# FFN2 of batches 5 and 6 by seven block products

## The chip, the cores and the metric

The kernel runs on one core of a Trainium2 chip. The time is microseconds (us) of one execution on the device; lower is better. The profile and the trace show one profiled execution, in which times count from the first instruction. Engines: PE multiplies matrices (PEld is its load of weights), DVE and ACT work on rows in on-chip memory and read PE's accumulators, POOL works on rows too but not on accumulators, SP issues output transfers.

## The reference

Inputs are q, k, v (8 batches x 8 heads x 576 x 64) and phi (8 x 8 x 576 x 32), and four weights. For each batch and head:

```python
a = softmax(phi, axis=2)                 # over the 576 rows
k_m, v_m = a.T @ k, a.T @ v              # 32 x 64
attn = softmax(q @ k_m.T / sqrt(64))     # 576 x 32
x = attn @ v_m                           # heads side by side: 4608 x 512 over all batches
h = maximum(maximum(x @ w1, x @ w2), x @ w3)   # 4608 x 768
out = h @ w_out                          # 4608 x 512
```

## The kernel before

All arithmetic on PE is in bf16 with 32-bit accumulators; outputs are 32-bit. The product with v_m is folded into the weights of each batch: `wp` holds v_m times (w1 - w3) and v_m times (w2 - w3), and `wp3` holds v_m times w3 times w_out. So h is kept as a difference to x @ w3 (`hT`, 768 columns in six tiles of 128, two batches side by side), and FFN2 adds attn @ wp3 to h @ w_out.

The order of all work is written out by hand: the long string that ends the kernel lists pieces such as F8@4, and each engine runs its own share of them in that order. The letter is the step, the number behind it the part, and the number behind @ the batch. A "!" swaps the engine of the step.

- L0 to L3 and H load phi, k, v and q; the issue is on POOL. E exponentiates phi on ACT. r0 and r1 (`pack`, L103) copy k and v from `kvo` into `kvr` beside a column of ones, on POOL, from batch 2 on.
- B (`att_kv`, L249) makes the key and value sums, N scales them on DVE, K transposes them. Q transposes q on DVE. S (`att_score`) makes the scores and two exponentials on ACT.
- a, s, c (DVE), m (POOL, `att_mul`, L409) and X (DVE) normalise the scores, in halves 0 and 1; X writes `attn`.
- D (`fold`, L440) folds v_m into the weights, in the parts 0 to 2 for `wp` and 3 for `wp3`; ACT or DVE takes the result out of the accumulators.
- F (`ffn1`, L466) is one of 12 pieces of FFN1 of a batch, four matmuls of 288 columns: an even number makes `h1` (evicted on ACT, L170), an odd one the other difference, which DVE joins to `h1` by a maximum into `hT` (L479).
- T0 to T3 (`ffn2`, L497 and L506) are tiles of 128 rows of a batch's output, T4 the 128 rows that two batches share, 64 of each. A tile is six matmuls of 512 columns on `hT` and two on `attn`, an eviction into `ot`, one of six buffers, and a transfer of 256 KB that SP issues. The last tile, T3@7, is made in two halves of 256 columns (`ffn2_last`, L538 and L546).

The eight banks of accumulators are dealt out by a second string of digits. A piece that gets a bank waits until its last user has been evicted.

Of the kernel before, what the change touches and what calls it, by code (L numbers as in the profile page):

```python
# [15 lines left out]
def kernel(  # L16
# [12 lines left out]
    nc = tc.nc  # L29
# [33 lines left out]
    kvos = []
    for i in range(2):
        kvo = const.tile([P, 3, NP, NC, D], BF16, name=f"kvo{i}")
        kvos.append(kvo)
# [28 lines left out]
    def load_kv(b, i, h=slice(0, NP)):
        kv = loaded.setdefault(b, {})["kv"] = kvos[b % 2]
        nc.gpsimd.dma_start(  # L97
            out=kv[:, 1 - i, h].rearrange("p j c d -> p j (c d)"),
            in_=by_pair((k, v)[i], b)[:, h],
        )  # L100

    def pack(b, i):
        nc.gpsimd.tensor_copy(  # L103
            out=kvrs[b % 2][:, :, :, D * i : D * (i + 1)], in_=kvos[b % 2][:, 1 - i]
        )
# [32 lines left out]
    banks = iter(  # L138
        "".join(
            """  # L140
            00224460026701101401264026402640264026452063420643064206420642064562074206742064
            20642064201640264102640264026402640264072406247026402640264024602406520462046204
            62704267402640264124602416420642064206420642067676767670
            """.split()
        )
    )
# [81 lines left out]
            s["e"] = work.tile([P, NP, NC, M], BF16, name="e")  # L228
        nc.scalar.activation(out=s["e"][:, js], in_=loaded[b]["ph"][:, js], func=AF.Exp)  # L229

    def k_and_ones(kv, r, j, c):

        flat = kv[r].rearrange("p i j c d -> p (i j c d)")
        k0 = (NP * NC + j * NC + c) * D
        step = 2 * NP * NC * D - k0
        return flat[:, k0 : k0 + 2 * step].rearrange("p (i x) -> p i x", i=2)[:, :, 0:D]

    def att_kv(b, part=None):
        s = st[b]
        kvp = two_banks()  # L240
        s["kvp", part] = kvp
        kv = loaded[b]["kv"]
        nd = {None: 2 * D + 1, 0: 2 * D, 1: D}[part]
        kvr = kvrs[b % 2]
        for c in range(NC):
            for j in range(NP):
                for a in range(NG):
                    r = slice(HP * a, HP * (a + 1))
                    nc.tensor.matmul(  # L249
                        kvp[M * j : M * (j + 1), a, 0:nd],  # L250
                        lhsT=s["e"][r, j, c, :],
                        rhs={
                            None: lambda: kvr[r, j, c, 0:nd],
                            0: lambda: k_and_ones(kv, r, j, c),
                            1: lambda: kv[r, 0, j, c, :],
                        }[part](),
                        start=(c == 0),
                        stop=(c == NC - 1),
                        tile_position=(HP * a, M * j),
                    )  # L260
# [102 lines left out]
    def ones_rec(b, g):  # L363
# [39 lines left out]
        s = st[b]  # L403
        nc.vector.reciprocal(out=s["sm", g], in_=s["sm", g])  # L404

    def att_mul(b, g):
        s = st[b]
        t = s["t", g]
        nc.gpsimd.tensor_tensor(  # L409
            out=t,  # L410
            in0=t,
            in1=s["sm", g].unsqueeze(2).to_broadcast([P, S // HP, R, 2]),
# [43 lines left out]
    def ffn1(b, n, swap):  # L456
# [20 lines left out]
        else:  # L477
# [83 lines left out]
    def issue(b, n, swap):  # L561
# [18 lines left out]
            "m": lambda: att_mul(b, i),  # L580
# [11 lines left out]


    for w in """
        E@0 H2@0 H0@0 L3@0 Z25@0 B0@0 Y2@0 I@0 N0@0 Z2@0 K0@0! Q0@0 Q1@0 Z9@0 S@0 Z2@0 M0@0 M1@0
        R0@0 R1@0 W0@0 Y3@0 W1@0 W2@0 Z6@0 O1@0 H3@0 O3@0 O2@0 H1@0 X1@0 B1@0 X0@0 N1@0
        K1@0 O0@0 Y0@0 D1@0! D0@0! D3@0 F8@0 F10@0 F2@0 V0@0 F6@0 F0@0! Y1@0 D2@0 D4@0 F4@0
        L0@1 V1@0 F1@0 E@1 F3@0 L1@1 F5@0 F9@0 F7@0 L3@1 F11@0 B0@1 T3@0 N0@1 K0@1! L2@1 Q1@1
        L2@2 L1@2 Q0@1 L0@2 V2@0 T0@0! L3@2 S@1 T1@0 a0@1 s0@1 c0@1 m0@1 B1@1 N1@1 a1@1 L1@3
        K1@1 s1@1 D0@1 D1@1! D2@1 c1@1 m1@1 X0@1 L3@3 r1@2 X1@1 T2@0! L2@3 F6@1 F10@1 F7@1 F2@1  # L600
        F3@1 F4@1 F0@1 r0@2 E@2 F5@1 F1@1 F11@1 L0@3 L0@4 F8@1 L2@4 F9@1 B@2 D3@1 N@2 Q1@2
        T0@1! K@2 T2@1! r0@3 Q0@2 S@2 a0@2 a1@2 s1@2 c1@2 m1@2 T4@1! D1@2! s0@2 D2@2 c0@2 m0@2
        X1@2 D0@2 T3@1 Q0@3 L3@4 X0@2 Q1@3 T1@1 F0@2 F4@2 F8@2 F6@2 F9@2 E@3 F7@2 r1@3 F5@2
        F10@2 F1@2 B@3 L1@4 D3@2 N@3 L0@5 F2@2 F11@2 E@4 F3@2 L1@5 K@3 r1@4 L2@5 T2@2! S@3 T3@2
        a0@3 s0@3 c0@3 m0@3 D0@3 D2@3 a1@3 s1@3 c1@3 X0@3 D1@3! Q0@4 m1@3 T1@2 L3@5 L2@6 T0@2!
        X1@3 F10@3 r0@4 F2@3 F4@3 E@5 Q1@4 r0@5 F5@3 F3@3 L1@6 F8@3 B@4 N@4 D3@3 F9@3 F6@3
        F11@3 L0@6 K@4 F0@3 F7@3 F1@3 S@4 a0@4 T4@3! s0@4 a1@4 D0@4 c0@4 s1@4 r1@5 c1@4 D3@4
        m0@4 X0@4 Q0@5 T0@3! D1@4! D2@4 B@5 T3@3 m1@4 X1@4 L0@7 F10@4 Q1@5 N@5 F8@4 K@5 F6@4
        F9@4 S@5 F7@4 L3@6 F2@4 F4@4 a0@5 L1@7 a1@5 F0@4 s0@5 r1@6 F3@4 D0@5 r0@6 s1@5 c1@5 E@6
        D3@5 m1@5 c0@5 F1@4 T1@3 L2@7 F11@4 L3@7 E@7 F5@4 m0@5 B@6 D1@5! D2@5 X1@5 N@6 T2@3!  # L610
        X0@5 F6@5 F8@5 Q0@6 Q1@6 K@6 F4@5 F9@5 S@6 F7@5 r0@7 a0@6 F2@5 a1@6 s0@6 c0@6 F0@5
        F10@5 m0@6 F1@5 s1@6 c1@6 F11@5 F5@5 T0@4! F3@5 X0@6 T2@4! r1@7 D0@6 D1@6! Q0@7 B@7
        m1@6 N@7 X1@6 T2@5! K@7 T3@4 Q1@7 S@7 a0@7 F2@6 s0@7 a1@7 s1@7 c1@7 m1@7 c0@7 F4@6
        T4@5! D3@6 D2@7 D0@7! T0@5! D3@7 D2@6 X1@7 m0@7 D1@7! T1@4 X0@7 F6@7 F3@6 T1@5 F4@7
        F8@7 F0@7 F5@6 F10@6 F7@7 F9@7 F10@7 F5@7 F0@6 F11@7 F6@6 F1@7 F7@6 F2@7 F8@6 F11@6
        F9@6 F1@6 F3@7 T0@6! T0@7! T3@5 T2@7! T2@6! T1@6 T1@7 T3@6 T4@7! T3@7
    """.split():
        n, b = w.rstrip("!").split("@")
        issue(int(b), n, w.endswith("!"))
# [30 lines left out]
```

## Time and profile before

| | us |
|---|---|
| median of 3 runs | 164.66 |
| lowest and highest run | 164.32, 165.99 |
| profiled execution, first to last instruction | 163.3 |
| PE busy | 153.8 |
| ACT busy | 100.6 |
| DVE busy | 90.4 |
| POOL busy | 69.5 |

A line of a group has the source line, the engine, the operation with its output and inputs, how many there were, then busy time in all and the mean of one in ns. "min/median/max" lines give ns of one. In the chain of waits a line is a start, a duration and what ran: the chain is followed back from the last instruction, at each step to what released it. Positions in the text are us from the first instruction.

### The profile page before, as it was taken

To read this page: it belongs to the slowest core of one execution; us is meant where nothing else is said; L and a number is where in the kernel's file an instruction comes from. 1 tells how busy PE (TensorE), PEld (TensorE's weight loads), DVE (VectorE), ACT (ScalarE), POOL (GpSimd) and SP (SyncE) were. 2 spreads that over 40 slices of the span, in tenths; PEclk is the share of its full clock that TensorE was granted. 3 is DMA by queue.
4 is the path that set the end of the run, shared out by engine and by line. 5 is a ranking of instruction groups with operands and counts; after the bars stand their busy time and mean duration, and the time that the engine had idled before them with its cause. 6 is when DMAs were issued, how large, how long until landed. Compare 5 with 4: busy or idle time off the path is not lost.

```text
span 163.3 us, 4838 instructions
## 1 busy us (share of the span) xinstructions
PE 153.8 (94%) x2080; PEld 85.3 (52%) x2080; DVE 90.4 (55%) x181; ACT 100.6 (62%) x151; POOL 69.5 (43%) x71
## 2 busy tenths in 40 slices
PE   7978798899899999999999999999999999999990
PEld 2433444564377436743673575576553468744450
DVE  2023704798838665849399748879749128810010
ACT  4205445845497488778885899994658976223320
POOL 7932205100599259657968957646403100000000
PEclk9999999999999999999999999999999999999998
DMA  6999999999999999999999999996313130014333
GB/s 150 152 206 207 205 210 217 274 208 210 253 313 238 209 253 379 274 210 293 252 263 206 232 355 264 191 233 150 130 69 129 69 128 0 0 68 186 135 128 130
DMA packets 21974, 31.77 MB, mean 195 GB/s; under 512 B 1216, under 2 KB 16576, under 8 KB 21952
## 3 DMA queue, kind: packets, MB, share of 16 engines
q0 software_dynamic: 16080, 21.43, 68.7%
q1 hardware_dynamic: 5728, 9.90, 17.2%
q8 instruction: 16, 0.26, 0.6%
q10 hardware_dynamic: 144, 0.13, 0.2%
q14 instruction: 6, 0.05, 0.1%
HBM read 39.32 MB, written 9.44 MB: 299 GB/s over the span
## 4 chain that ended last, share of the span: by engine, by line
PE 83%; DMA 9%; POOL 2%; ACT 2%; issue 1%; DVE 1%; ACTq 0%; POOLq 0%
PE psum L497 29%; PE psum L466 28%; DMA wo_sb<-in_moe_w_out_dram 9%; PE psum L506 8%; PE psum L440 6%; PE psum L249 4%; PE psum L192 3%; PE psum L333 2%; PE psum L515 1%; ACT h L170 1%; PE psum L538 1%; PE psum L298 1%; POOL kvo L97 1%; ACT wp L172 1%; POOL qq L110 0%
## 5 line engine op out<-in xcount | busy, mean ns | idle before, releaser
L497 PE MATMUL psum<-wo_sb,hT 128*128 128x512 bf16 x210 | 51.3, 380 | 0.0
L466 PE MATMUL psum<-attn,wp 128*128 128x288 bf16 x384 | 50.5, 286 | 0.1
L479 DVE TENSOR_TENSOR hT<-psum,h 128x576 bf16<-128x576 f32 x48 | 34.2, 749 | 18.0 <-PE psum L466 12.5
L466 PEld LDWEIGHTS <-wp 128*128 128x128 bf16 x384 | 36.7, 98 | 13.2 <-issue 2.0
L172 ACT COPY ot<-psum 128x512 f32<-128x512 f32 x35 | 20.7, 591 | 32.1 <-PE psum L506 25.2
L497 PEld LDWEIGHTS <-hT 128*128 128x128 bf16 x210 | 19.2, 97 | 24.0 <-issue 4.3
L172 ACT CAST wp<-psum 128x1024 bf16<-128x1024 f32 (+1 forms) x31 | 29.2, 995 | 3.8 <-PE psum L440 2.0
L103 POOL COPY kvr<-kvo 128x2304 bf16<-128x2304 bf16 x12 | 25.3, 2111 | 13.7 <-DMA kvo<-in_k_dram 10.1
L170 ACT ACTIVATE h<-psum 128x576 bf16<-128x576 f32 x47 | 28.4, 659 | 3.5 <-PE psum L466 3.3
L409 POOL TENSOR_TENSOR t<-t,sm 128x576 bf16<-128x576 bf16 x14 | 16.1, 1154 | 24.6 <-DVE sm L404 24.4
L506 PE MATMUL psum<-wp,attn 128*128 128x512 bf16 x62 | 18.4, 379 | 0.0
L159 PE MATMUL psum<-warm 128*128 128x512 bf16 x44 | 12.1, 427 | 1.2 <-DVE warm L128 1.2
L313 DVE STREAM_TRANSPOSE qT<-qq 128x576 f32<-128x576 f32 x16 | 11.7, 747 | 1.4 <-DMA qq<-in_q_dram 1.4
L342 ACT ACTIVATE e<-psum 128x576 bf16<-128x576 f32 x16 | 9.6, 652 | 3.8 <-PE psum L333 3.8
L229 ACT ACTIVATE e<-ph 128x1152 bf16<-128x1152 f32 (+1 forms) x9 | 9.6, 1065 | 1.7 <-DMA ph<-in_phi_dram 1.6
L395 DVE TENSOR_REDUCE sm<-t 128x18 f32<-128x576 bf16 x14 | 10.3, 738 | 0.2
L387 DVE STREAM_TRANSPOSE t<-e 128x288 f32<-128x288 f32 x14 | 6.4, 465 | 6.2 <-ACT e L342 6.1
L97 POOL DMA_DIRECT2D kvo<-in_v_dram x9 | 6.7, 749 | 7.1 <-PE psum L249 4.1
L506 PEld LDWEIGHTS <-attn 128*128 128x128 bf16 x62 | 6.1, 98 | 7.1
L110 POOL DMA_DIRECT2D qq<-in_q_dram x8 | 6.2, 770 | 6.6 <-DVE h L174 3.7
L555 DVE COPY ot<-psum 128x256 f32<-128x256 f32 x1 | 0.4, 425 | 15.4 <-PE psum L546 15.4
L249 PEld LDWEIGHTS <-e 64*32 64x32 bf16 x720 | 6.9, 90 | 3.7 <-issue 3.3
(57 smaller groups left out, 114.4 us busy)
## 6 DMA issues: line engine op xcount, KB each, us to landing
out_dram<-ot SPq DMA_DIRECT2D x35, 256.0 KB, 5.6
qq<-in_q_dram POOLq DMA_DIRECT2D x8, 576.0 KB, 12.2
ph<-in_phi_dram POOLq DMA_DIRECT2D x7, 576.0 KB, 14.4
kvo<-in_k_dram POOLq DMA_DIRECT2D x7, 576.0 KB, 14.6
kvo<-in_v_dram POOLq DMA_DIRECT2D x7, 576.0 KB, 15.6
w_sb<-in_moe_w_dram POOLq DMA_DIRECT2D x3, 768.0 KB, 19.0
wo_sb<-in_moe_w_out_dram POOLq DMA_DIRECT2D x1, 768.0 KB, 14.6
ph<-in_phi_dram SPq DMA_DIRECT2D x2, 288.0 KB, 3.0
```

What stands on the lines that cost most here:

```text
L103: nc.gpsimd.tensor_copy(out=kvrs[b % 2][:, :, :, D * i : D * (i + 1)], in_=kvos[b % 2][:, 1 - i])
L159: nc.tensor.matmul(po[:, 0:BANK], lhsT=warm[:, 0:P], rhs=warm, start=True, stop=True)
L170: nc.scalar.activation(out=out_, in_=in_, func=AF.Relu)
L172: nc.scalar.copy(out=out_, in_=in_)
L249: nc.tensor.matmul(kvp[M * j : M * (j + 1), a, 0:nd], lhsT=s["e"][r, j, c, :], rhs={None: lambda: kvr[r, j, c, 0:nd], 0: lambda: k_and_one ...
L313: nc.vector.transpose(out=s["qT"][:, j].rearrange("p j c r e -> p (j c r e)").bitcast(FP32), in_=loaded[b]["q"][:, j].rearrange("p j c d - ...
L395: nc.vector.tensor_reduce(out=sm, in_=s["t", g].rearrange("p n r e -> p n e r"), op=ALU.add, axis=mybir.AxisListType.X,)
L409: nc.gpsimd.tensor_tensor(out=t, in0=t, in1=s["sm", g].unsqueeze(2).to_broadcast([P, S // HP, R, 2]), op=ALU.mult,)
L466: nc.tensor.matmul(acc[:, h, 0:SH], lhsT=wps[b][:, g, w * DF + ft * P : w * DF + (ft + 1) * P], rhs=attn[:, g, c0 : c0 + SH], start=(g == ...
L479: nc.vector.tensor_tensor(out=hT[:, ft, (b % 2) * S : (b % 2 + 1) * S].rearrange("p (h n) -> p h n", h=2), in0=a, in1=s["h1", ft], op=ALU.max,
L497: nc.tensor.matmul(po, lhsT=hT[:, fc, c0 : c0 + P], rhs=wo_sb[:, fc, :], start=(n == 0), stop=False,)
L506: nc.tensor.matmul(po, lhsT=attn[:, g, c0 : c0 + P], rhs=wp3s[b][:, g, :], start=False, stop=(g == NG - 1),)
```

## The change

For batches 5 and 6 the tiles T0 to T3 go. Their 512 rows by 512 columns are taken as two by two blocks: rows in the two parities r of 128-row tiles (256 rows each), columns in halves of 256, and the inner dimension in two halves of four tiles, three of h and one of attn. Seven products of blocks, in place of eight, give the four blocks of the output, with sums and differences of blocks of h and attn (A) and of the weights (U) made beforehand. U@9 makes those of w_out once, in the room of `w3T`; U@5 and U@6 make those of `wp3`, which differ by batch. The sums of h lie in the room of w3 and, for A2, in `hT` itself; A0 to A3 are those of h (768 columns), A4 to A7 those of attn (256).

A product P is eight matmuls of 256 columns, for two row tiles into the halves of one bank. Three banks are used for a batch: P1, P4, P5 and P6 add up in one, P0 and P3 in another, and P2 has the third. After P0, P1 and P4 a copy of the bank is kept (`snap`, 512 columns of 32 bits), and the output is one plain copy and three adds of a bank and a snapshot on DVE, into `oj0` and `oj1`, of 512 KB each, which one transfer each takes out.

Beside this, the pack can be made on ACT (used for r1@7), A runs on DVE without "!" and on POOL with it, U the other way round, output buffers `ot` fall from six to four, `kvo` loses an unused third, the string of banks is new, and the order is new from the piece after F7@2 on. Before that it is the same.

```diff
-    opool = ctx.enter_context(tc.tile_pool(name="opool", bufs=6))
+    opool = ctx.enter_context(tc.tile_pool(name="opool", bufs=4))
...
-    def pack(b, i):
-        nc.gpsimd.tensor_copy(
-            out=kvrs[b % 2][:, :, :, D * i : D * (i + 1)], in_=kvos[b % 2][:, 1 - i]
-        )
+    def pack(b, i, swap):
+        out_, in_ = kvrs[b % 2][:, :, :, D * i : D * (i + 1)], kvos[b % 2][:, i]
+        if swap:
+            nc.scalar.copy(out=out_, in_=in_)
+        else:
+            nc.gpsimd.tensor_copy(out=out_, in_=in_)
...
+    SNAP = {0: "m5", 1: "m1", 4: "u2"}
...
+    def combine(on_dve, out_, in0, in1, op):
+        eng = nc.vector if on_dve else nc.gpsimd
+        eng.tensor_tensor(out=out_, in0=in0, in1=in1, op=op)
+
+    def combine_w(b, i, on_dve):
...
+        in0, in1 = [(x[B12], x[B11]), (x[B22], t[0]), (x[B22], x[B12]), (x[B21], t[1])][i]
+        combine(on_dve, t[i], in0, in1, SUB)
...
+    def combine_a(b, i, on_dve):
+
+        s, sa = sums(b)
+        n = i % 4
+        if i < 4:
+            (a11, a12), (a21, a22) = blocks(hts[b // 2], b, KT)
+            t = {0: s[:, 0], 1: s[:, 1], 2: a21, 3: s[:, 2]}
+        else:
+            (a11, a12), (a21, a22) = blocks(attns[b // 2], b, 1)
+            t = {m: sa[:, m : m + 1] for m in range(4)}
+        in0, in1 = [(a21, a22), (t[0], a11), (a11, a21), (a12, t[1])][n]
+        combine(on_dve, t[n], in0, in1, ADD if n == 0 else SUB)
+
+    def products(b, i, swap):
...
+        lhs, rhs, name = [
+            (summed(0), w_summed(0), "y"),
+            (plain(0, 0), w_plain(0, 0), "x"),
+            (plain(0, 1), w_plain(1, 0), "z"),
+            (summed(3), w_plain(1, 1), "y"),
+            (summed(1), w_summed(1), "x"),
+            (summed(2), w_summed(2), "x"),
+            (plain(1, 1), w_summed(3), "x"),
+        ][i]
...
+        for k in range(KT + 1):
+            for q in range(2):
+                nc.tensor.matmul(
+                    po[:, q * CH : (q + 1) * CH],
+                    lhsT=lhs(k, q),
+                    rhs=rhs(k),
+                    start=(i < 3 and k == 0 and q == 0),
+                    stop=(k == KT and q == 1),
+                    skip_group_check=True,
+                )
...
+        if i in SNAP:
+            t = ln if i == 0 else work.tile([P, S], FP32, name="snap", tag="r")
+            t = acc[SNAP[i]] = t[:, 0:DM].rearrange("p (q n) -> p q n", q=2)
+            copy(t, x)
...
+        done = [2] if i == 2 else [i] if i > 4 else [4] if 3 in acc and 4 in acc else []
+        for n in done:
+            ot = acc["ot"][n // 5][:, :, slice(0, CH) if n in (2, 6) else slice(CH, DM)]
+            if n == 6:
+                copy(ot, x)
+            else:
+                if n == 4:
+                    x = acc["y"].rearrange("p (q n) -> p q n", q=2)
+                y = acc[{2: "m1", 4: "u2", 5: "m5"}[n]]
+                nc.vector.tensor_tensor(out=ot, in0=x, in1=y, op=ADD)
+            if n in (4, 6):
...
+                nc.sync.dma_start(out=rows[:, :, n // 5], in_=acc["ot"][n // 5])
...
-            "r": lambda: pack(b, i),
+            "r": lambda: pack(b, i, swap),
...
+            "U": lambda: combine_w(b, i, swap),
+            "A": lambda: combine_a(b, i, not swap),
+            "P": lambda: products(b, i, swap),
...
+        Q1@3 T1@1 F0@2 F4@2 F8@2 F6@2 F9@2 E@3 F7@2 F1@2 L1@4 r1@3 F10@2 F2@2 L2@5 B@3
+        N@3 D3@2 F3@2 L1@5 F5@2 K@3! U0@9 F11@2 S@3 U1@9 E@4 T3@2 L0@5 T0@2! a1@3 D1@3!
+        s1@3 D2@3 a0@3 r1@4 c1@3 L3@5 D0@3 T1@2 m1@3 s0@3 Q0@4 X1@3 c0@3 m0@3 X0@3 T2@2!
+        F4@3! r0@4 F5@3 L2@6 F0@3 D3@3 B@4 F6@3 N@4 F1@3 F8@3 Q1@4 F2@3 F9@3 K@4! F10@3
+        r1@5 F7@3 S@4 F11@3 L3@6 D3@4 E@5 r0@5 F3@3 a0@4 U3@9 L0@6 a1@4 T4@3! L1@6 L0@7
+        s1@4 D0@4 D1@4! B@5 c1@4 N@5 T1@3 Q1@5 K@5 L1@7 Q0@5 s0@4 c0@4 m0@4 T3@3! S@5
+        a0@5 T2@3! s0@5 a1@5 c0@5 X0@4 m1@4 X1@4 D2@4 D0@5 D1@5 m0@5 s1@5 X0@5 T0@3!
+        F4@4 c1@5 F2@4 m1@5 r1@6 L2@7 F10@4 r0@6 F3@4 F5@4 F8@4 X1@5 F9@4 F0@4 F11@4
+        F6@4 E@6 F10@5! F7@4 L3@7 F0@5 F2@5 A4@5! Q0@6 A5@5! F1@4 F1@5 A7@5! F8@5 F6@5
+        F4@5! Q1@6 D3@5 B@6 N@6 r0@7 D2@5 T0@4! F7@5 F5@5 K@6 F3@5 U2@9 F9@5 U0@5! T1@4!
+        F11@5 A0@5 A6@5 r1@7! E@7 S@6 T2@4! D1@6! U1@5! D2@6 a0@6 Q1@7 B@7 A1@5! U2@5
+        U3@5 N@7 T3@4 s0@6 K@7! Q0@7 a1@6 P1@5 D3@6 s1@6 c1@6 S@7 c0@6 A2@5! m1@6 P2@5
+        P4@5 a0@7 s0@7 D3@7 D2@7 m0@6 a1@7 c0@7 D1@7! P0@5! A3@5! U0@6 s1@7 P5@5 c1@7
+        m1@7 X1@6 X0@6 T4@5! D0@6! D0@7 P6@5 U1@6 m0@7 F8@6 F9@6 F6@6 U3@6 U2@6 X0@7
+        P3@5 F10@6 F2@6 X1@7 F11@6 F8@7 F0@6 F3@6 F7@6 F4@7 F1@6 F9@7 F4@6 A4@6 F5@6
+        F2@7 F0@7 F5@7 A0@6! A6@6! A1@6! F6@7 F10@7! F3@7 A5@6! P1@6 A2@6! F1@7 P0@6
+        F7@7 A3@6! F11@7 P2@6! P4@6 T0@7 T1@7 P5@6! A7@6 T4@7 P6@6! P3@6! T2@7! T3@7
```

More of the change, by code (lines that the diff above doesn't have):

```diff
@@ L62 @@
     nc.scalar.preload_act_table_set("natural_log_exp_and_others")
[L63 to L66, printed above, removed]
+    KV = NP * NC * D
+    ones_k = [const.tile([P, D + 2 * KV], BF16, name=f"kvo{i}") for i in range(2)]
+    kvos = [
+        x[:, D:].rearrange("p (i j c d) -> p i j c d", i=2, j=NP, c=NC) for x in ones_k
+    ]
     kvrs = [
@@ L128 @@
     nc.vector.memset(warm, 0.0)
-    for kvo in kvos:
-        nc.vector.memset(kvo[:, 2, 0, 0], 1.0)
+    for x in ones_k:
+        nc.vector.memset(x[:, 0:D], 1.0)
     blkones = const.tile([P, P], BF16, name="blkones")
@@ L280, in att_kv_norm @@
             return
+        k0 = D if part == 0 else 0
         for g in range(NG):
@@ L370, in ones_rec @@
         )
-        r = work.tile([P, S], FP32, name="r")
+        r = work.tile([P, S], FP32, name="r", tag="r")
         nc.scalar.activation(out=r, in_=ln, func=AF.Exp, scale=-1.0)
@@ L484, in ffn1 @@
             )
+    KT = FT // 2
+    CH = DM // 2
+    TW = 2 * P
+    SUB, ADD = ALU.subtract, ALU.add
+    B11, B12, B21, B22 = [
+        (slice(KT * i, KT * (i + 1)), slice(CH * j, CH * (j + 1)))
+        for i in range(2)
+        for j in range(2)
+    ]
+    tw = w3T.rearrange("p f j n -> p (f j n)").rearrange("p (i k c) -> p i k c", i=4, k=KT)
+    sa0 = const.tile([P, 4, TW], BF16, name="sa0")
+    oj0 = [const.tile([P, 2, DM], FP32, name=f"oj{i}") for i in range(2)]
+    SNAP = {0: "m5", 1: "m1", 4: "u2"}
@@ new lines @@
+    twb, sas, quads = {}, {}, {}
+    def combine(on_dve, out_, in0, in1, op):
+        eng = nc.vector if on_dve else nc.gpsimd
+        eng.tensor_tensor(out=out_, in0=in0, in1=in1, op=op)
+    def combine_w(b, i, on_dve):
+        if b == B + 1:
+            x = {n: wo_sb[:, n[0], n[1]] for n in (B11, B12, B21, B22)}
+            t = [tw[:, n] for n in range(4)]
+        else:
+            if b not in twb:
+                twb[b] = work.tile([P, 4, CH], BF16, name="twb")
+            w = wp3s[b]
+            x = {n: w[:, n[0].start // KT, n[1]] for n in (B11, B12, B21, B22)}
+            t = [twb[b][:, n] for n in range(4)]
+        in0, in1 = [(x[B12], x[B11]), (x[B22], t[0]), (x[B22], x[B12]), (x[B21], t[1])][i]
+        combine(on_dve, t[i], in0, in1, SUB)
@@ L601 @@
[L601 to L612, printed above, removed]
```

118 lines of the change are left out of this document (90 added, 28 removed).

## Prediction

> **What bounds the kernel now.** I read the page's summary first, then the chain of waits in order of time, then the busy time by stretches, and last the queues that the change loads. The page says one engine is nearly full, and the chain says the end follows that engine:
>
> ```profile
> span 163.3 us, 4838 instructions
> PE 153.8 (94%) x2080; PEld 85.3 (52%) x2080; DVE 90.4 (55%) x181; ACT 100.6 (62%) x151; POOL 69.5 (43%) x71
> PE 83%; DMA 9%; POOL 2%; ACT 2%; issue 1%; DVE 1%; ACTq 0%; POOLq 0%
> ```
>
> A busy PE need not be PE at its limit, so the pieces of the chain matter more (start, duration, what):
>
> ```profile
> 28.96 1.75 ACT h L170 x3
> ...
> 43.23 0.17 DVE kvt L176
> 43.41 0.04 issue
> 43.45 0.84 PE psum L440 x24
> ...
> 81.78 0.73 PE psum L249 x71
> 82.51 0.23 PE psum L440 x8
> ...
> 84.32 0.17 PE psum L298 x3
> ...
> 85.95 0.41 PE psum L333 x23
> ...
> 91.47 0.65 PE psum L249 x69
> 92.12 1.40 PE psum L497 x6
> 93.52 0.43 PE psum L506 x2
> ...
> 100.27 1.29 PE psum L497 x6
> 101.57 0.43 PE psum L506 x2
> ...
> 116.63 0.65 PE psum L249 x69
> ...
> 132.27 9.80 PE psum L466 x80
> ...
> 157.18 0.55 PE psum L515 x4
> 157.73 0.76 PE psum L538 x6
> 158.49 0.22 PE psum L546 x2
> 158.71 0.66 PE psum L538 x6
> ```
>
> From 43.45 on the chain holds PE work alone, but for one 0.02 us of issue. Each piece starts where the last ended. Waits of other engines lie before that, where the order of pieces isn't changed. By stretches (length, then busy time of each engine and its instructions, clock, DMA share, GB/s):
>
> ```profile
> 70.00:115.00 45.00, 44.98 (x685) 25.95 (x684) 34.63 (x72) 36.31 (x53) 32.17 (x26) 1.00 1.11 238
> 115.00:159.60 44.60, 44.58 (x412) 24.24 (x410) 17.54 (x32) 23.86 (x37) 3.42 (x4) 1.00 0.26 98
> 159.60:163.30 3.70, 0.00 (x0) 0.00 (x0) 0.00 (x0) 0.37 (x1) 0.00 (x0) 0.78 0.32 109
> ```
>
> PE is full in both, at clock 1.00. In 70 to 115 DVE, ACT and POOL have 20 to 30% left and DMA none; after 115 all four have room. So less PE work shortens the run, as long as nobody else falls behind in 70 to 115.
>
> **The products on PE.** FFN2 of one 128-row tile is six matmuls on h and two on attn, 1.29 + 0.43 = 1.72 us; the 1.40 stands where a piece follows matmuls of 64 rows, and the 0.11 more is the price of entry. The change takes out four such tiles in each of batches 5 and 6: 8 x 1.72 = 13.76 us. It puts in 14 products of eight matmuls of 256 columns. The trace has that very form, in the last tile, which is made in halves: 0.66 + 0.22 = 0.88 us for eight, 110 ns each, each with a weight load of its own. 14 x 0.88 = 12.32 us, so PE loses 1.44 us. Seven products in place of eight leave 7/8 of the columns; of the time 12.32 / 13.76, 0.895, are left, so the smaller matmuls give little of it back. Entries: in both orders 27 runs of narrow matmuls (key sums, scores, folds) are followed by full ones, so none is gained or lost.
>
> To place pieces in the new order I add prices along it: an FFN1 piece 0.49 (9.80 for twenty), a tile 1.72, the shared one of two batches 1.29 + 0.55 = 1.84, a product 0.88, key sums 0.73, a fold 0.23, scores 0.41, transposes 0.17, and 0.11 for each entry. Only differences of such sums are used below.
>
> [...]
>
> **What the products need from the others.** Prices, from the forms:
>
> ```profile
> L103 POOL COPY kvr<-kvo x12: 2102/2108/2124, 46.4 to 112.9; 128x2304 bf16<-128x2304 bf16 x12
> L409 POOL TENSOR_TENSOR t<-t,sm x14: 1147/1152/1174, 42.4 to 126.2; 128x576 bf16<-128x576 bf16 x14
> L377 DVE TENSOR_TENSOR attn<-e,r x2: 749/750/751, 18.4 to 19.1; 128x576 bf16<-128x576 bf16 x2
> L479 DVE TENSOR_TENSOR hT<-psum,h x48: 694/748/758, 32.7 to 142.6; 128x576 bf16<-128x576 f32 x48
> L172 ACT COPY ot<-psum x35: 585/586/632, 37.7 to 157.8; 128x512 f32<-128x512 f32 x35
> L229 ACT ACTIVATE e<-ph 128x1152 bf16<-128x1152 f32 x7 | 8.2, 1174 | 0.0
> ```
>
> Evictions: a batch had four copies of 586 ns; it gets three snapshots and one plain copy of that size, so nothing is added there, and three adds on DVE, by L479 0.748 x 512/576 = 0.67 us each, 2.0 us a batch. Most lie after 115, where DVE is busy 17.54 of 44.60. They stand on PE's path only where a product adds onto a bank that is still being read. In batch 5, P4 follows P1's snapshot with a fold, scores and P2 between; in batch 6, F1, P0, F7, F11 and P2 stand there (four times 0.49 to 0.88), against a copy of 0.59. P6 of batch 6 has one T4, 1.84, to cover an add of 0.67. I take nothing; uncovered, each costs at most its 0.6 to 0.7.
>
> Sums and differences of weights and of h: 11 of 768 columns and 11 of 256 fall to POOL. Their form isn't in the trace. Between the copy (0.92 ns a column) and the multiply (2.0) I take 2.0, as it also reads two inputs: 1.54 and 0.51 us, 22.6 us in all; the low end is 10.3. Some 18 of that lies in the last 55 us, where POOL has little to do (3.42 in the last 44.60). On DVE come one of 768 and five of 256, at 1.30 ns a column by L377 at most 2.7 us. The tightest deadline: A0@5 can run once h of batch 5 is whole, A1@5 follows it on POOL (1.0 + 1.54), and P4@5, which needs both, stands 7.9 us behind A0@5 by the PE prices. In batch 6, A0, A6, A1 and A5 stand on POOL ahead of P4, 2 x 1.54 + 2 x 0.51 = 4.1 us, and P4 stands 5.6 us behind A0. Both are covered, the second by 1.5 less what DVE owes at that time.
>
> Loads: U0 and U1 of the output weights stand on POOL ahead of L0@5 and r1@4, 3.1 us; U3 ahead of L0@6, L1@6, L0@7, L1@7, 1.5 us. What covers it is that loads queue behind each other anyway:
>
> ```profile
> kvo<-in_k_dram POOLq DMA_DIRECT2D x7, 576.0 KB, 14.6
> kvo<-in_v_dram POOLq DMA_DIRECT2D x7, 576.0 KB, 15.6
> ```
>
> They take 15 us from issue to landing with 16 engines full, so a load that joins the queue 3 us later lands when it would have, if the queue isn't empty. One load is really moved back: phi of batch 5 now stands behind keys and values of that batch, 5.0 us of transfer (two of 576 KB at the 238 GB/s of 70 to 115), and its exponential stands 5.9 us of PE work later than it did. Covered by 0.9. The pack r1@7 goes to ACT: by 1174 ns for 1152 columns, 2.35 us there against 2.11 on POOL; that is a rival below.
>
> Staging: four output buffers in place of six. Landing is 5.6 us in the median, 7.6 at worst:
>
> ```profile
> out_dram<-ot SPq DMA_DIRECT2D x35, 256.0 KB, 5.6
> DMA to landing us min/median/max: 2.0/5.6/7.6
> out_dram<-ot SPq DMA_DIRECT2D x1, 128.0 KB, 1.7
> ```
>
> The closest five tiles in the new order are T0, T2, T4, T3, T1 of batch 1: the fifth ends 8.5 us behind the first, and a copy, an issue of 0.3 and 5.6 are 6.5. At the worst landing, 8.5: just enough. At the end two outputs of 512 KB join: 0.3 us more for each 128 KB (1.7 to 2.0) makes 1536 KB 3.6 us of transfer, issued over some 5 us. Nothing, and 0.5 at most. The kernel still ends with the halves of T3@7, so the 3.7 us behind the last matmul stay.
>
> **The sum.** Span 163.3 - 1.44 = 161.9. I add 0.1 for new short waits: 162.0. The median is 1.36 above the span (164.66 - 163.3), so 163.3.
>
> **Rivals.**
>
> *Slower: ACT waits for the values of batch 7.* The pack r1@7 needs that load; with it on ACT, everything behind it on ACT waits too: E@7, both exponentials of S@6, then T2@4's copy and the folds D1@6, D2@6. On POOL in the kernel before:
>
> ```profile
> 102.15 0.81 POOL L97 DMA_DIRECT2D kvo<-in_v_dram  x1
> ...
> 112.92 2.11 POOL L103 COPY kvr<-kvo 128x2304 bf16<-128x2304 bf16 x1
> ```
>
> The pack waited for nothing, so the load landed within 10.8 us. In the new order the load stands behind m1@5 and the pack r1@6. B@7 (key sums of batch 7), the first to need the pack, stands 1.7 us later in the sum of PE work than in the old order, at 116.63 + 1.7 = 118.3. F2@4, next to m1@5, stands 18.8 us of PE work ahead of that, at 99.5; m1@5 (1.15) and the pack (2.11), with 1.7 more for waits, put the load's issue at 104.5, an estimate. Landing within 10.8 it is there by 115.3, and the pack ends by 117.7. Room 0.6. If it took the median of 15.6, the pack would end at 122.4 and B@7 start 4.1 late: 164.66 - 1.44 + 4.1 = 167.3. It decides once the landing takes over 11.5 us. For it: the DMA share is 1.11. Against it: this is the last load but one, and the queue runs dry behind it. Chance 0.10.
>
> *Some of the gain is given back.* PE meets short waits in 70 to 125, since DVE (34.63 of 45) and ACT (36.31) are the next fullest there and the new order has moved many of their pieces: two to four waits of 0.3 to 0.6 us cost 0.6 to 2, so 163.9 to 165.2. Chance 0.22.
>
> *The products are no cheaper.* If each paid an entry as the first half does (0.76 against 0.66), 14 x 0.98 = 13.72 us, and nothing is gained: 164.6. Against it: the second half, right behind the first, paid none. Chance 0.05.
>
> *More than the sum.* Another 0.6 us of waits or entries goes: 162.6. The chain shows nothing to win past 43.45. Chance 0.05.
>
> **How the numbers follow.** The forecast, a clean gain of 1.44 with waits up to 0.5, has the rest, 0.58, and gives 162.8 to 163.8; its middle is the predicted time. A measurement here can tell about 1% from no change, so faster means below 163.0 and slower above 166.3. Of the clean case nearly two fifths fall below 163.0 (the three runs before lie between 164.32 and 165.99), 0.22, and with the 0.05 faster has 0.27, say 0.28. Slower is the first rival and a tail of the second, 0.12; 0.60 is left within 1%. The range 162.6 to 165.2 leaves out the slow rival and the outermost tails.
>
> **What would show it.** Right: L497 with 162 matmuls in place of 210, products of eight at 0.88 us, a chain of PE alone past 43, a span near 162.0. Wrong: a piece "ACT kvr" or "DMA kvo" in the chain near 111 to 122 (the pack), "POOL sa" or "POOL s" ahead of P0 or P4, "DVE ot" or "ACT snap" ahead of a product, or an "ot" copy that waits for an output's landing.

## The result and the profile after

| | us |
|---|---|
| before, median of 9 runs (lowest, highest) | 165.28 (164.32, 165.99) |
| after, median of 9 runs (lowest, highest) | 163.59 (163.16, 164.42) |
| ratio after / before, 95% interval | 0.9919 (0.9894 to 0.9943) |
| profiled execution after, first to last instruction | 162.4 |

The change makes the kernel 0.8% faster, by 0.6 to 1.1%. The profiled execution after is one of the two slowest of its nine; their spans lie between 161.2 and 162.5, the median at 161.7. (In e11 below, the ratio leaves out the four slowest of twelve runs, the profiled one among them; so it is smaller than that of the medians, and the wait in that trace need not be the typical one.)

From the summary page after: the span, the engines' busy time with instruction counts, the chain's shares by engine, and the group of FFN2's tile matmuls on h (busy time, mean ns of one, idle time before), with the same group of the kernel before beneath. Lines of the kernel after have new numbers: L250 is the key sums, L300 their transposes, L335 the scores, L344 their exponentials, L442 the fold, L468 FFN1, L658 and L667 the tiles, L600 the products, L505 their sums, L175 and L179 the evictions on ACT and DVE.

```profile
span 162.4 us, 4946 instructions
PE 152.6 (94%) x2128; PEld 90.5 (56%) x2128; DVE 104.5 (64%) x201; ACT 97.8 (60%) x144; POOL 92.2 (57%) x92
PE 62%; DMA 27%; DVE 4%; POOL 3%; ACT 1%; issue 1%; POOLq 0%
L658 PE MATMUL psum<-wo_sb,hT 128*128 128x512 bf16 x162 | 39.6, 380 | 0.0
```

```profile
L497 PE MATMUL psum<-wo_sb,hT 128*128 128x512 bf16 x210 | 51.3, 380 | 0.0
```

PE loses 1.2 us of busy time, DVE and POOL gain 14 and 23, and PE still is the full one. The tiles' matmuls on h are 162, as against 210 before. The chain has new links, so it is read piece by piece (start, duration, what ran):

```profile
27.17 24.16 DMA ph<-in_phi_dram
...
51.36 1.17 ACT e L232
...
52.58 0.80 PE psum L250 x69
...
70.75 0.49 ACT kvt L175
...
71.28 0.48 PE psum L335 x26
...
115.78 0.69 DVE ot L179
...
117.93 1.67 DVE twb L505
...
121.03 0.53 DVE kvn L285 x2
...
121.60 0.28 PE psum L300 x2
121.89 0.87 PE psum L600 x8
...
145.75 1.75 PE psum L600 x16
```

Three things are to be seen. First, a product is 0.87 us, two of them 1.75: the eight matmuls cost what the half tile's eight did. Second, PE now waits at two places behind 52.58: 0.07 us for ACT's copy of the transposed keys at 71.28, and 0.05 us for DVE at 121.60. The chain runs over DVE for almost 6 us before the second, but PE worked all that time; the wait is the part that counts. Third, the chain breaks off at the key sums of batch 2 (52.58), which waited for phi of batch 2. That load landed at 51.34 in this execution and at 50.03 in the one before, and its issue lies ahead of the first changed piece; in the experiments below, whose work up to there is that of the kernel after, it landed between 49.6 and 51.0. So it belongs to the execution, not to the change.

For that reason the two traces are compared from the start of batch 2's key sums on. The window view, from there to the last matmul (length, then busy time of PE, PEld, DVE, ACT and POOL with instructions, clock, DMA share, GB/s), before:

```profile
51.94:159.58 107.64, 107.62 (x1403) 60.47 (x1402) 64.64 (x130) 73.22 (x109) 46.50 (x38) 1.00 0.76 186
```

and after:

```profile
52.58:158.99 106.41, 106.29 (x1450) 65.56 (x1450) 78.42 (x149) 70.83 (x102) 69.12 (x59) 1.00 0.76 185
```

The stretch is shorter by 107.64 - 106.41 = 1.23 us; the 3.73 us behind the last matmul became 3.41. Counting each matmul from its own start to the start of the next, the tiles fell from 53.11 to 39.15 us and 14 products came for 12.45: 1.51 us less. All the rest up to the last matmul grew by 0.28, of which the two waits are 0.12.

Nearly all of the 0.3 us saved behind the last matmul lies behind the landing of the last output: from there to the end are 1.51 us before and 1.22 after. In e1 and e5 below, which have the tiles too, it is 1.50; in all kernels with products 1.04 to 1.22. So some 0.3 us of the gain is not PE time. No run shows what it is.

### The profile page after: what moved, and what is told of

It reads as the page before. It is cut to its first block, busy times and chain, and to the rows that moved or that the text cites. A ratio compares the mean times of both kernels' runs of the same rounds, so it can differ in the third digit from the quotient of the medians.

```text
span 162.4 us, 4946 instructions
## 1 busy us (share of the span) xinstructions
PE 152.6 (94%) x2128; PEld 90.5 (56%) x2128; DVE 104.5 (64%) x201; ACT 97.8 (60%) x144; POOL 92.2 (57%) x92
## 4 chain that ended last, share of the span: by engine, by line
PE 62%; DMA 27%; DVE 4%; POOL 3%; ACT 1%; issue 1%; POOLq 0%
PE psum L468 22%; PE psum L658 17%; DMA ph<-in_phi_dram 15%; DMA w_sb<-in_moe_w_dram 12%; PE psum L600 8%; PE psum L667 5%; PE psum L442 4%; PE psum L250 2%; POOL kvo L98 2%; PE psum L676 1%; PE psum L335 1%; DVE twb L505 1%; PE psum L699 1%; ACT e L232 1%; PE psum L300 1%
## 5 line engine op out<-in xcount | busy, mean ns | idle before, releaser
L468 PE MATMUL psum<-attn,wp 128*128 128x288 bf16 x384 | 50.2, 286 | 0.2
L468 PEld LDWEIGHTS <-wp 128*128 128x128 bf16 x384 | 36.9, 98 | 12.0 <-issue 1.5
L658 PE MATMUL psum<-wo_sb,hT 128*128 128x512 bf16 x162 | 39.6, 380 | 0.0
L173 ACT ACTIVATE h<-psum 128x576 bf16<-128x576 f32 x43 | 26.1, 657 | 7.2 <-PE psum L468 7.1
L175 ACT CAST wp<-psum 128x1024 bf16<-128x1024 f32 (+1 forms) x30 | 28.4, 996 | 2.6 <-PE psum L442 2.6
L175 ACT COPY ot<-psum 128x512 f32<-128x512 f32 x23 | 13.6, 591 | 23.2 <-PE psum L667 18.2
L108 POOL COPY kvr<-kvo 128x2304 bf16<-128x2304 bf16 x11 | 23.2, 2111 | 5.5 <-DMA kvo<-in_k_dram 4.4
L658 PEld LDWEIGHTS <-hT 128*128 128x128 bf16 x162 | 14.6, 98 | 17.8 <-issue 3.2
L667 PE MATMUL psum<-wp,attn 128*128 128x512 bf16 x46 | 13.7, 379 | 0.0
L344 ACT ACTIVATE e<-psum 128x576 bf16<-128x576 f32 x16 | 9.6, 653 | 6.1 <-PE psum L335 6.1
L250 PEld LDWEIGHTS <-e 64*32 64x32 bf16 x720 | 7.1, 90 | 4.5 <-issue 2.8
L98 POOL DMA_DIRECT2D kvo<-in_k_dram x9 | 6.9, 769 | 2.9 <-DMA qq<-in_q_dram 2.1
L419 DVE STREAM_TRANSPOSE attn<-t 128x288 f32<-128x288 f32 x14 | 6.2, 456 | 3.5 <-POOL t L411 3.5
```

The source lines that it names most:

```text
L98: nc.gpsimd.dma_start(out=kv[:, i, h].rearrange("p j c d -> p j (c d)"), in_=by_pair((k, v)[i], b)[:, h],)
L108: nc.gpsimd.tensor_copy(out=out_, in_=in_)
L173: nc.scalar.activation(out=out_, in_=in_, func=AF.Relu)
L175: nc.scalar.copy(out=out_, in_=in_)
L468: nc.tensor.matmul(acc[:, h, 0:SH], lhsT=wps[b][:, g, w * DF + ft * P : w * DF + (ft + 1) * P], rhs=attn[:, g, c0 : c0 + SH], start=(g == ...
L658: nc.tensor.matmul(po, lhsT=hT[:, fc, c0 : c0 + P], rhs=wo_sb[:, fc, :], start=(n == 0), stop=False,)
```

## The experiments

All but e3 keep the kernel after but for the edit; e3 has the order of before. The edits are shown in part ("..." marks a cut). Where pieces change places (e1 to e5 and e12), the string of banks is new too, and A and U go or come with their products; so these runs test an order together with its banks. "B2 to end" is the stretch from batch 2's key sums to the last matmul in the profiled execution.

| run | median us | ratio to before (95%) | B2 to end us |
|---|---|---|---|
| before | 165.28 | 1 | 107.64 |
| after | 163.59 | 0.9919 (0.9894 to 0.9943) | 106.41 |
| e1 tiles, new order | 166.47 | 1.0063 (1.0038 to 1.0087) | 109.13 |
| e5 tiles, placed otherwise | 166.05 | 1.0050 (1.0024 to 1.0075) | 108.57 |
| e2 products of batch 6 only, new order | 164.91 | 0.9966 (0.9945 to 0.9988) | 107.81 |
| e3 products of batch 6 only, old order | 164.52 | 0.9936 (0.9911 to 0.9961) | 107.15 |
| e4 products of batch 7 too | 164.30 | 0.9941 (0.9916 to 0.9966) | 105.86 |
| e12 as e4, outputs in quarters | 164.41 | 0.9939 (0.9917 to 0.9960) | 106.11 |
| e6 values of batch 7 behind r0@7 | 170.79 | 1.0310 (1.0260 to 1.0360) | 114.49 |
| e11 values of batch 7 behind L3@7 | 167.82 | 1.0099 (1.0062 to 1.0137) | 110.95 |
| e8 pack r1@7 on POOL | 163.98 | 0.9912 (0.9883 to 0.9941) | 106.33 |
| e7 U1@5 next to U0@5 | 163.84 | 0.9918 (0.9889 to 0.9947) | 106.57 |
| e9 no sums | 163.51 | 0.9890 (0.9851 to 0.9929) | 106.11 |
| e10 three buffers | 164.86 | 0.9971 (0.9949 to 0.9994) | 107.60 |

### Products or order: e1, e2, e3, e5

Is the gain the products' alone? e1 puts the tiles of both batches back at places of the products, in the new order, without sums; e2 does so for batch 5 only.

```diff
...
-        Q0@7 a1@6 P1@5 D3@6 s1@6 c1@6 S@7 c0@6 A2@5! m1@6 P2@5
-        P4@5 a0@7 s0@7 D3@7 D2@7 m0@6 a1@7 c0@7 D1@7! P0@5! A3@5! U0@6 s1@7 P5@5 c1@7
-        m1@7 X1@6 X0@6 T4@5! D0@6! D0@7 P6@5 U1@6 m0@7 F8@6
+        Q0@7 a1@6 T0@5! D3@6 s1@6 c1@6 S@7 c0@6 m1@6 T1@5
+        a0@7 s0@7 D3@7 D2@7 m0@6 a1@7 c0@7 D1@7! T2@5! s1@7 c1@7
+        m1@7 X1@6 X0@6 T4@5! D0@6! D0@7 m0@7 F8@6
...
```

> The new order, staging and pack, with the tiles T0 to T3 of batches 5 and 6 back in the places of P1, P4, P0, P3 (batch 5) and P1, P2, P5, P3 (batch 6), and without the sums. Theory (the gain is PE time of the products alone, and the new order only hides what they need): 8 x 1.72 us in place of 14 x 0.875 us, 1.5 us more than the changed kernel, so a ratio to the kernel before of 0.998 to 1.003. Rival (the new order is what gains): it stays near 0.992. Second rival (the new order costs something of its own, and the products gain more than 1.5): above 1.004.

> The changed kernel with tiles in batch 5 and products in batch 6 alone. Theory: half the gain, 4 x 1.72 - 7 x 0.875 = 0.75 us, a ratio of 0.995 to 0.997, and the POOL sums of batch 5 missing from 107 to 128 us give nothing more. Rival (the products of batch 5, in the full stretch, lose by waits what they gain): 0.992, as good as both batches.

e1 came out at 1.0063, outside my theory's range and in that of the second rival: tiles in the new order are slower than tiles in the old one, though PE has the same matmuls. e2 came out at 0.9966, inside its range, but not by the sum that gave the range: from e1 to e2 the ratio falls by almost 1%, where 0.75 us would be 0.45%, and e2 still has waits ahead of FFN1 pieces like the two below, of 0.17 and 0.32 us. A cost of the order and a larger gain offset each other there. The chain of e1 shows where PE stands:

```profile
129.46 0.67 issue
130.13 0.59 ACT ot L175
130.72 0.98 ACT wp L175
131.69 0.04 issue
131.74 1.14 PE psum L468 x8
```

The FFN1 pieces behind the folds D0@6 and D0@7 need a bank and a fold that ACT hands over behind the copy of T4@5. In the kernel after, P6@5 stands between the folds and these pieces and covers it. In all PE waits 0.9 us behind batch 2's key sums in e1, 0.12 after. e5 places the tiles with more care (T0@5 in the place of P2, T1@5 of P0, T2@5 of P6).

> The first experiment again, tiles in the new order, but placed where they cover what the products covered: T0 to T3 of batch 5 stand at P2, P0, P6 and P3, those of batch 6 at P1, P0, P2 and P4. Theory (the 1.0 us of waits in the first experiment came from taking away the pieces ahead of F8@6 and F11@7, not from the new order itself): these waits are gone from the chain, 1.0 to 1.5 us less than there, a ratio of 0.997 to 1.001 to the kernel before, and the products are worth their PE time, 1.5 us. Rival (the new order costs 1 us of its own, which the products repay): 1.004 or more.

This theory fell too: 1.0050, in the rival's range. Those waits are gone, but S@7 now waits 0.55 us at 123.24 for ACT's copy of batch 7's transposed keys, where T0@5 no longer stands. The chain of e5:

```profile
122.70 0.49 ACT kvt L175
...
123.24 0.49 PE psum L335 x25
```

My reading, which no run tests by itself: seven pieces of 0.88 cover more gaps than four of 1.72, and the new order is cut for seven. e3 asks the same from the other side: the order of before, with products in batch 6, whose tiles lie at the end.

```diff
...
-        F9@6 F1@6 F3@7 T0@6! T0@7! T3@5 T2@7! T2@6! T1@6 T1@7 T3@6 T4@7! T3@7
+        m0@7 U0@9 U1@9 U3@9 U2@9 U0@6 U1@6 U3@6 U2@6 D1@7! T1@4 X0@7 F6@7 F3@6 T1@5 F4@7 F8@7
...
+        A4@6 A0@6! A6@6! A1@6! A5@6! A2@6! A3@6! F3@7 T3@5 P1@6 T0@7! P0@6 P2@6! P4@6 T2@7!
+        P5@6! A7@6 T1@7 P6@6! T4@7! P3@6! T3@7
```

> The order of the kernel before, untouched up to the last FFN1 pieces, with products for batch 6 alone: the sums run on POOL past 127 us, where it had nothing to do, and only the last ten pieces are rearranged. Theory: 0.75 us less PE work, of which waits at the tail take up to 0.4: a ratio of 0.995 to 0.998. Rival (without the new order the products bring nothing): 0.999 or more, with a wait of PE on POOL or DVE ahead of a product in the chain.

The ratio, 0.9936, is lower than the 0.995 to 0.998 expected. One batch's products give 0.64% in the old order, 1.06 us (0.64 to 1.47), where the PE prices come to 0.72 a batch; in the traces B2 to end falls by 0.49. So in batch 6 the products need no new order. In the new order the step from tiles to products in both batches is 166.47 - 163.59 = 2.9 us, or 2.5 against e5. By B2 to end it is 2.7 and 2.2: 1.5 of PE work, 0.8 and 0.5 of the waits named above, and 0.4 and 0.1 that are not traced. Products of both batches in the old order weren't tried.

### More of the same: e4, e12

e4 makes products in batch 7 too; T4@7 is then the last piece, in halves. Its 512 KB outputs use buffers (`ox`) that are free by then.

```diff
...
-        F7@7 A3@6! F11@7 P2@6! P4@6 T0@7 T1@7 P5@6! A7@6 T4@7 P6@6! P3@6! T2@7! T3@7
+        F7@7 A3@6! F11@7 P2@6! A0@7 P4@6 A1@7 P1@7 P5@6! A7@6 A2@7! P0@7 A3@7 P6@6!
+        P3@6! P4@7 P2@7! P5@7! P3@7 P6@7 T4@7!
```

> The changed kernel with products for batch 7 too, its sums on POOL and DVE in the tail, and T4 of batch 7 last, in halves. PE loses another 4 x 1.77 - 7 x 0.875 = 0.95 us, and the halves of T4 pay 0.1 to 0.2 for their extra matmuls of 64 rows. Theory: the end follows PE, so 0.5 to 0.8 us less than the changed kernel, a ratio of 0.986 to 0.989. Rival (the last outputs of 512 KB, four of them in the last 8 us, or the sums of batch 7, hold up the end): 0.991 or more, with a DMA or a POOL sum in the chain past 145 us.

PE's stretch does become shorter, by 0.55 us, but the kernel doesn't: 0.9941. The time is the rival's, its sign is not: past 145 us the chain holds PE alone up to the last eviction, so no DMA or sum holds PE up. What is lost lies behind the last matmul. DMA issues from 150 us on (KB each, median us from issue to landing), after:

```profile
out_dram<-ot SPq DMA_DIRECT2D x4, 256.0 KB, 2.0
out_dram<-oj SPq DMA_DIRECT2D x2, 512.0 KB, 3.1
...
out_dram<-ot ACTq DMA_DIRECT2D x1, 128.0 KB, 1.8
```

and e4:

```profile
out_dram<-ox SPq DMA_DIRECT2D x2, 512.0 KB, 3.7
...
out_dram<-ot ACTq DMA_DIRECT2D x1, 128.0 KB, 2.5
```

The last 128 KB take 2.5 us instead of 1.8, and the end stands 4.02 us behind the last matmul instead of 3.41. From batch 2's key sums to the end it is 105.86 + 4.02 = 109.88, after 106.41 + 3.41 = 109.82. Products hand their rows out at the end of the batch, in large pieces. e12 tests whether smaller and earlier ones help.

```diff
...
-            if n in (4, 6):
+            if b == B - 1:
+                c = slice(0, CH) if n in (2, 6) else slice(CH, DM)
+                nc.sync.dma_start(out=rows[:, :, n // 5, c], in_=ot)
+            elif n in (4, 6):
...
```

> The kernel with products for batches 5, 6 and 7, whose last matmul came 0.76 us earlier but whose end stood 4.02 us behind it (3.41 in the changed kernel); now batch 7's 512 KB outputs go as four of 256 KB, each as soon as its quarter is formed. Theory (that version gave its gain back to outputs that queue behind each other in the last microseconds): the last output lands 3.3 to 3.5 us behind the last matmul, span 161.6 to 161.9, ratio to the kernel before 0.987 to 0.990. Rival (the four outputs, in lines of 1 KB instead of 2 KB, take the engines as long or longer in all): 3.9 us or more behind it, ratio 0.993 to 0.996.

The rival was right: 4.26 us behind the last matmul, 0.9939. DMA issues of e12 from 150 us on:

```profile
out_dram<-ox SPq DMA_DIRECT2D x4, 256.0 KB, 4.0
```

256 KB take 4.0 us, longer than 512 KB in e4, and twice the 2.0 us of the tiles' 256 KB after. Whether the shorter lines or the queue behind batch 6's outputs does it, these runs don't separate. Neither version beats the kernel after.

### The late values: e6, e11, e8

The prediction's slow rival was a late load of batch 7's values in front of the pack on ACT. In the kernel after it is issued at 103.88 and lands at 111.84; ACT's rows:

```profile
111.92 0.59 ACT L175 COPY ot<-psum 128x512 f32<-128x512 f32 x1 [0.74 <-PE psum L667]
112.40 2.12 ACT L106 COPY kvr<-kvo 128x2304 bf16<-128x2304 bf16 x1
```

The pack starts right behind a tile's copy and waits for nothing. e6 moves that load's issue behind the pack r0@7:

```diff
-        m1@5 r1@6 L2@7 F10@4 r0@6
+        m1@5 r1@6 F10@4 r0@6
...
-        B@6 N@6 r0@7 D2@5
+        B@6 N@6 r0@7 L2@7 D2@5
```

> The changed kernel with the load of the values of batch 7 issued behind the pack r0@7, at some 111.7 us in place of 103.9. The slow rival of the prediction says: it lands 6.5 to 8 us later than the issue, 118.2 to 119.7; the pack on ACT ends 2.1 later, B@7 starts 1.5 to 3 us late, and what ACT holds behind the pack (E@7, the exponentials of S@6) is 4 to 5 us late, so 2 to 5 us slower than the changed kernel, a ratio to the kernel before of 1.004 to 1.022, with the load in the chain of waits. If ACT's wait is covered, it stays at 0.992.

The load lands 15.6 us behind its old issue (119.50 for 103.88), just what the rival was priced for: 167.3 us, 1.016 of the 164.66 then known. It costs more, 1.031, beyond the 1.022 that I expected at most, and PE stands elsewhere. The chain of e6:

```profile
112.00 7.50 DMA kvo<-in_v_dram
...
121.60 1.16 ACT e L232
122.75 1.09 ACT e L344 x2
...
123.88 1.05 PE psum L442 x12
124.93 0.98 PE psum L250 x70
```

PE stands 5.99 us ahead of L442, the fold D1@6, and not ahead of B@7 (L250), which follows it. D1@6 needs the banks of S@6's scores, whose exponentials stand on ACT behind the pack and E@7. From landing to fold are 4.38 us. If so, a landing between this one and that of the kernel after must cost by the same rule; e11 issues the load behind that of the queries.

```diff
-        m1@5 r1@6 L2@7 F10@4 r0@6
+        m1@5 r1@6 F10@4 r0@6
...
-        F7@4 L3@7 F0@5
+        F7@4 L3@7 L2@7 F0@5
```

> The load of batch 7's values issued on POOL behind the pack of batch 6 and the load of queries of batch 7: about 107.8 instead of 103.9, to land at 115 to 116. Theory as the late-values run left it (TensorE stands at the fold D1@6 until the landing plus 4.4 us, by way of the pack, E@7's copy and S@6's exponentials on ACT, and would come there at 118.4 by itself): a wait of 1.0 to 2.0 us ahead of the fold, ratio to the kernel before 0.998 to 1.004. Rival (the threshold of the prediction, landing more than 11.5 us after an issue at 104.5, that is at 116.0, at B@7): no wait, ratio 0.990 to 0.994.

The chain of e11:

```profile
107.35 9.45 DMA kvo<-in_v_dram
...
121.19 0.98 PE psum L442 x16
122.17 0.97 PE psum L250 x72
123.15 2.20 PE psum L658 x6
```

The load landed a little later than I had put it, at 116.80, and PE resumed 4.39 us behind it, after a wait of 3.21. Wait and ratio (1.0099) are above what I expected, but the place and the 4.4 us are those of the theory. The prediction's threshold, 116.0, would leave a wait of 0.8, at B@7. Landing less wait gives the limit: 116.80 - 3.21 = 113.6 here and 119.50 - 5.99 = 113.5 in e6. In the kernel after, whose batch 2 starts 0.5 to 0.7 us later than in these two, PE comes to the fold at 118.40 (PE's rows):

```profile
117.87 0.59 PE L667 MATMUL psum<-wp,attn 128*128 128x512 bf16 x2
118.40 0.62 PE L442 MATMUL psum<-w_sb,kvt 64*32 64x512 bf16 x16
```

So its limit is 118.40 - 4.39 = 114.0, and the landing at 111.84 leaves 2.2 us. e8 puts the pack back on POOL (r1@7 without "!").

> The changed kernel with the pack r1@7 on POOL, as all others. POOL has it between U2@9 and A1@5, where it had nothing to do from 113.3 to 117.8 us. Theory: the pack on ACT had 4 us of room and costs nothing, and it costs nothing on POOL either: 0.990 to 0.994. Rival: ACT is the next bound in that stretch, and 2.1 us less on it make S@6 and what follows earlier: 0.988 or less.

0.9912: where the load is in time, the pack on ACT costs nothing. The 4 us of room in this expectation were 2.2.

### What stands beside PE: e9, e7, e10

e9 leaves out the block sums; the products read plain blocks.

```diff
...
-            src = h[1][0] if n == 2 else s[:, min(n, 2)]
-            return lambda k, q: src[:, k, q] if k < KT else sa[:, n, q]
+            return plain(1, n % 2)
...
-            return lambda k: tw[:, n, k] if k < KT else twb[b][:, n]
+            return w_plain(n % 2, 1)
...
```

> Left out: all 28 block sums and differences (the products read plain blocks instead, so the output isn't the reference's); the fourteen products, their evictions and outputs stay. Theory (the 25 us of sums on POOL and the 4 us on DVE lie wholly beside TensorE's work): ratio to the kernel before 0.990 to 0.993, as with them (0.9919), the stretch from B@2 to the last matmul 106.2 to 106.5 us (106.42 with them). Rival 1 (the sums hold evictions up and so cost several tenths): 0.987 to 0.989 and 105.6 to 106.0 us. Rival 2 (the bare products are no cheaper than with sums because the output copies of the products are the limit): no change and new waits ahead of the products.

B2 to end is 106.11, below my theory's range by 0.1 and above the rival's by as much, and the ratio's interval holds both. No PE wait stands ahead of a product, so the second rival is out. The three runs with sums and no other cost (after, e7, e8) lie between 106.33 and 106.57. So the 28 sums cost 0.2 to 0.5 us at most; how much of that is real, one trace against three can't tell.

One sum is odd. DVE after (start, duration, line, operation) has the second difference of `wp3`, U1@5, as its last line here:

```profile
117.17 0.56 DVE L505 TENSOR_TENSOR w_sb<-hT 128x768 bf16<-128x768 bf16 x1
117.64 0.29 DVE L505 TENSOR_TENSOR sa<-attn 128x256 bf16<-128x256 bf16 x1
117.84 1.75 DVE L505 TENSOR_TENSOR twb<-wp,twb 128x256 bf16<-128x256 bf16 x1
```

and POOL at that time:

```profile
117.81 1.64 POOL L505 TENSOR_TENSOR w_sb<-w_sb,hT 128x768 bf16<-128x768 bf16 x1 [4.52 <-DVE w_sb L505]
```

Like operations take 0.28 us on DVE. e7 makes U1@5 earlier, while POOL has no such operation.

```diff
...
-        U0@5! T1@4! F11@5 A0@5 A6@5 r1@7! E@7 S@6 T2@4! D1@6! U1@5! D2@6
+        U0@5! U1@5! T1@4! F11@5 A0@5 A6@5 r1@7! E@7 S@6 T2@4! D1@6! D2@6
```

> The changed kernel with U1@5, on DVE, moved ahead by a few instructions, directly behind U0@5, to 115.7 us, where POOL has nothing to do. In the changed kernel it stood beside the POOL difference A1@5 and took 1.75 us, where like operations of its size took 0.28. [...] Rival (its operands, of which one is the output of U0, make it slow): 1.7 us here too. The time changes by less than 0.3 us either way, since PE waited only 0.05 us behind it: a ratio of 0.990 to 0.993.

DVE in e7:

```profile
115.80 0.29 DVE L505 TENSOR_TENSOR twb<-wp,twb 128x256 bf16<-128x256 bf16 x1
```

0.29 us, and the wait at 121.60 is gone, but the time is the same, 0.9918. e10 takes away one more output buffer (`bufs=4` to `bufs=3` of `opool`).

> Three output staging buffers in place of four, nothing else. Theory (four are just enough, as the prediction had it: with outputs landing 6 us after their issue at 90 to 106, a tile's copy must now wait for the output three tiles before): waits of TensorE or of the copies of 0.3 to 2 us between 90 and 110, ratio to the kernel before 0.993 to 1.003. Rival (one buffer to spare, since only the tiles of batches 4, 6 and 7 use the staging): 0.990 to 0.993, no wait on an output that reaches TensorE.

0.9971, in the theory's range. One row of the waits (us in all, how often, longest), and the chain:

```profile
ACT ot L175 <- DMA out_dram<-ot: 0.8, 1, 0.8
```

```profile
98.99 0.99 PE psum L468 x8
...
99.99 0.59 ACT ot L175
...
100.63 2.43 PE psum L468 x18
```

A tile's copy waits 0.8 us for an output that has not landed, and PE stands 0.66 us ahead of an FFN1 piece. Three are too few; with four no copy waits for an output.

## Why the prediction was right

- **What bounds.** PE was, and is: 106.29 of 106.41 us from batch 2's key sums on. The sign "a chain of PE alone past 43" did not come, but the waits that the new links bring PE are 0.12 us.
- **The products on PE.** The sum, -1.44 us, measured -1.51. What is left over goes to small waits and joints, +0.28, where I took 0.1: a net of -1.23 for -1.34.
- **The number.** 163.59 for 163.3 is closer than its parts. The 3.7 us behind the last matmul did not stay but became 3.41, which no term held, so the median span is 161.7 and not 162.0. The time was put 1.36 above the span; in the nine runs after it is 1.8 to 2.0 above, and the 164.66 of three runs before became 165.28 with nine. The two errors, 0.3 down and some 0.5 up, partly cancel, which is luck.
- **The price of a matmul.** The trace has 1.75 us for 16 matmuls of 256 columns, 109 ns each, where the nearest form of before, the last tile's halves, had given 110: the trace of before priced them well.
- **Evictions.** No product waits for a snapshot or an add. The adds measured 0.69 us, 0.67 was taken.
- **Sums.** Mis-sized: on POOL 1.64 and 0.67 us, where I took 1.54 and 0.51, so 11 x 2.31 = 25.4 us and not 22.6. On DVE they were cheaper, 0.56 and 0.28 for 1.00 and 0.33, but one took 1.75 beside POOL, which no term of mine held: 3.4 us in all, where I had 2.7 at most. By e9 all of them together cost 0.5 us at most.
- **Staging.** "Just enough" held: three buffers are too few (e10), and the kernel after has no such wait.
- **The slow rival.** It didn't occur, since the load landed 8.0 us after its issue. But its step was wrong: I put the deadline at B@7, "the first to need the pack". It is the fold D1@6 ahead of it, by way of a bank that ACT frees behind the pack, so the limit is a landing at 113.5 to 114.0 and not at 116.0 (e6, e11), and behind waits of 3.2 and 6.0 us there the granted clock was 0.50 for two and four microseconds (below). With the landing that the prediction took at the latest, 115.3, PE would have stood up to 115.3 + 4.39 - 118.40 = 1.3 us at the fold, an estimate. That the rival stayed away was luck in part. The pack, 2.12 us, was priced at 2.35; that was the smaller error.
- **What it left out.** The new order was taken as neutral. With tiles it is 0.5 to 0.6% slower than the old one (e1, e5), and with products PE's waits are 0.12 us: the products fill its gaps.

## What to carry to other kernels

Where PE is full, price smaller matmuls by the same form in the same trace; here 1.51 us less matmul time gave 1.23, beside helpers that had room. Find the deadline of a late transfer by following every engine's queue behind it, above all who holds an accumulator bank, and not the first reader alone. Work taken off the end pays only until the outputs themselves set the end: in e4 PE's stretch fell by 0.55 us, and the time to the end did not (109.88 for 109.82).

## What the runs showed of the hardware

**Waits of 3.21 and 5.99 us cost more than their length.** Windows of e11 around the fold's late start (the last three numbers are granted clock, DMA share, GB/s):

```profile
117.90:121.20 3.30, 0.09 (x5) 0.10 (x5) 1.77 (x3) 3.30 (x5) 3.30 (x4) 1.00 0.00 0
121.20:122.20 1.00, 1.00 (x40) 0.66 (x47) 0.56 (x1) 0.83 (x2) 0.66 (x1) 0.56 0.00 0
122.20:123.20 1.00, 1.00 (x73) 0.80 (x53) 0.01 (x1) 1.00 (x2) 0.00 (x0) 0.50 0.69 260
123.20:124.20 1.00, 1.00 (x3) 0.31 (x3) 0.96 (x5) 0.51 (x1) 0.00 (x0) 0.50 0.07 18
124.20:125.20 1.00, 1.00 (x5) 0.36 (x4) 1.00 (x3) 0.00 (x0) 0.00 (x0) 0.73 0.00 0
125.20:126.20 1.00, 1.00 (x10) 0.73 (x9) 0.97 (x3) 0.38 (x1) 0.00 (x0) 1.00 0.00 0
```

While PE stood for 3.21 us, the clock was 1.00. Behind that it was 0.56 in the first microsecond, 0.50 in the next two, 0.73 in the fourth and 1.00 in the fifth, and six matmuls took 2.20 us instead of 1.29 to 1.40. B2 to end grew by 4.54 us for a wait of 3.21; e6 by 8.08 for 5.99. Two windows of e6, the wait and the first microsecond behind it:

```profile
117.90:123.90 6.00, 0.02 (x7) 0.03 (x7) 1.69 (x3) 4.33 (x5) 3.85 (x4) 0.83 0.09 29
123.90:124.90 1.00, 1.00 (x33) 0.53 (x39) 0.56 (x1) 0.73 (x2) 0.00 (x0) 0.50 0.00 0
```

The mean over the 6 us of e6's wait is 0.83, so the clock was below 1.00 in a part of it, and 0.50 in each of the four microseconds behind it. e10, with a wait of 0.66 us, has a mean of 1.0 over its whole execution. What lowers the clock, and after how long, these runs don't show.

**A DVE operation beside one of POOL.** U1@5 took 1.75 us beside a POOL operation of 1.64, and 0.29 away from it (e7). POOL's had started 0.03 us earlier, and U1@5 ended 0.14 us after it had ended. Why it took that long, no run shows.
